# A fused attention and SwiGLU kernel: leftover tokens as half-size products, sums split between two engines, loads moved within a batch

## The chip, the cores and the metric

The kernel runs on one core of a Trainium2 chip. A core has a matrix engine (TensorE, PE in the profile, with PEld for its weight loads), a vector engine (VectorE, DVE), a scalar engine (ScalarE, ACT), a general engine (GpSimd, POOL) and a queue engine (SyncE, SP). Each runs its own instruction list in order and waits for others by semaphores. DMA transfers are issued from POOL, SP and ACT. The metric is the time of one execution in microseconds on the device: before the change a median of 237.15 us over three runs, 236.67 to 237.42.

## The reference

Eight batches, eight heads, 576 tokens, head size 64, 32 memories; then a SwiGLU block of width 512 with 1536 inner features over all 4608 tokens.

```python
def _attn_ref(q, k, v, phi):
    a = phi - np.max(phi, axis=2, keepdims=True)
    a = np.exp(a)
    a = a / (np.sum(a, axis=2, keepdims=True) + 1e-09)
    k_m = np.einsum('bhsm,bhsd->bhmd', a, k)
    v_m = np.einsum('bhsm,bhsd->bhmd', a, v)
    scores = (1.0 / np.sqrt(q.shape[-1])) * np.matmul(q, k_m.transpose(0, 1, 3, 2))
    attn = softmax(scores)
    return np.matmul(attn, v_m)

def _moe_ref(x, w_gate, w_val, w_out):
    g = x @ w_gate
    silu = g * (1.0 / (1.0 + np.exp(-g)))
    return silu * (x @ w_val) @ w_out
```

x is the attention's output with its heads side by side. Inputs and output are float32; the kernel computes in bfloat16 with float32 sums.

## The kernel before, in words

**A batch.** For batch b the kernel exponentiates phi (`phi_exp`), multiplies it with k and v (`kv_sum`, L235, into the tiles p_kv), divides by the column sums (`kv_denominators` L263, `kv_reciprocal`, `kv_norm` L271) and transposes the result into t_kT (`kv_T`). The values are folded into the gate and value weights (`u_round`, L471, evacuated to t_U by ScalarE L491 and VectorE L495). Scores come from q (transposed to t_qT by a DMA on SP) and t_kT (`scores`, L400); ScalarE takes their exponential (L411), VectorE sums and inverts it (`z_inv_v`: L434, L441, L443) and multiplies (`norm`, L451), once for each half g of the heads. This gives t_A, twice a batch.

**Slots.** The gate and value products of a batch run as 24 slots (12 blocks of 128 features, two halves of 288 tokens). `gv_gate` multiplies for the gate and ScalarE applies SiLU (t_sg, L531); one slot later the value product comes and VectorE multiplies both into t_h (L537). Three chunks c of four blocks make one tile t_h each. When a chunk is complete, `chunk_done` is called.

**Products.** The last multiplication, by w_out, uses a seven-product scheme for 2 x 2 blocks (four sums of activations, four of weights). It covers the first 512 of the 576 tokens of a batch: two halves of 256 tokens, with the features taken as even and odd blocks. `chunk_done` makes the activation sums t_S (L601 and, by `subtract`, L559: t[:, 0] = A21 + A22, t[:, 1] = t[:, 0] - A11, t[:, 2] = A11 - A21, t[:, 3] = A12 - t[:, 1]); for c = 0 and 1 GpSimd does this, for c = 2 VectorE. `products` lays out seven products of six units (a unit is two matmuls of 256 columns, L706): first (p1 and the one added to it), five, six, three, seven, four. They add up in the banks p_os, p_oa and p_oc, and `keep`, `c11`, `c22`, `c12`, `c21` copy and add them out and store them. A unit is not run at once: it goes into `backlog`, and `take(n)` runs the next n.

**Leftover tokens.** The last 64 tokens of each batch are copied by GpSimd (`ends`, L591) into xs of a pair of batches, t_x, 128 rows. `out_rest(pair, half)` multiplies them plainly by half of w_out: 12 matmuls of 256 columns in six units (L654), eight such passes in all.

**The order of the work** is written by hand. An iteration b of the last loop starts with 36 units of the former batch's products, with the scores, the softmax and `u_values` between them; then the 24 slots with what is spread between them: `kv_items(b + 1)` at slots 7 to 11 (with `u_item(b, 2)` behind it), `u_three(b + 1)` at 19 to 20, and the rest of the backlog from slot 4 on. GpSimd's list holds, in an iteration from 3 on: the loads of batch b + 2 (`loads`, L93, L98, L102, L115, four DMA issues), the last copy of leftover tokens, `phi_sum(b + 1)` (a sum over phi behind a mark that waits for t_A, L215 and L217, which makes the denominators two matmuls in place of nine), the sums and copy of c = 0, the sums and copy of c = 1. In iteration 2 the loads stand in the slots and there is no `phi_sum`. SP's list holds stores, the t_qT transposes and, from batch 4 on, the t_kT transposes. Eight banks of PSUM are handed out in order of release (`bank`, `done`).

Of the kernel before, what the change touches and what calls it, by code (L numbers as in the profile page):

```python
# [9 lines left out]
FP32 = mybir.dt.float32  # L10
# [4 lines left out]
def kernel(  # L15
# [193 lines left out]
    def phi_sum(b):  # L209

        e = ephis[b].rearrange("p j i m -> p j (i m)")
        mark = att.tile([1, 1], BF16, tag="mark", bufs=1, name="t_mark")
        nc.gpsimd.tensor_copy(out=mark, in_=atts[b - 1, 1][0:1, 0, 0:1])  # L215
        t = att.tile([128, 4, 128], FP32, tag="es", bufs=1, name="t_es")
        add = lambda o, x, y: nc.gpsimd.tensor_tensor(out=o, in0=x, in1=y, op=ALU.add)  # L217
        add(t, e[:, 0:4], e[:, 4:8])
        add(t[:, 0:2], t[:, 0:2], t[:, 2:4])
        add(t[:, 0], t[:, 0], t[:, 1])  # L220
        add(t[:, 0], t[:, 0], e[:, 8])
        hl = att.tile([128, 2, 128], BF16, tag="ehl", bufs=1, name="t_ehl")
        nc.gpsimd.tensor_copy(out=hl[:, 0], in_=t[:, 0])
        nc.gpsimd.tensor_tensor(out=hl[:, 1], in0=t[:, 0], in1=hl[:, 0], op=ALU.subtract)
        esums[b] = hl
# [71 lines left out]
    def kv_items(b, beside=None):  # L297


        def run_sums():  # L300
            o = 2 * D
            p = [bank([128, CH], FP32, f"p_kv{g}") for g in range(NG)]
            kv_denominators(b, p[0][:, o:o + NG])
            kv_sum(b, p, (0, 1))
            kv_reciprocal(b, p[0][:, o:o + NG])
            kv_norm(b, p)
            done(*p)
            if beside:
                beside()

        return [run_sums, lambda: kv_T(b)]
# [273 lines left out]
    def chunk_done(b, c):  # L585

        if b % 2 == 0 and c == 0:
            xs[b // 2] = hpool.tile([128, NJF, 2, 64], BF16, tag="xs", name="t_x")

        def ends():  # L590
            nc.gpsimd.tensor_copy(  # L591
                out=xs[b // 2][:, 4 * c:4 * c + 4, b % 2], in_=hts[b, c][:, :, S - 64:S]
            )

        t = upool.tile([128, 4, 2, 256], BF16, tag=f"U{c}" if b == 1 else f"S{c}", name="t_S")
        Ss[b, c] = t
        A11, A12, A21, A22 = blocks(b, c)

        def sums(eng, part=(0, 1, 2, 3)):
            if 0 in part:  # L600
                eng.tensor_tensor(out=t[:, 0], in0=A21, in1=A22, op=ALU.add)  # L601
            terms = ((t[:, 0], A11), (A11, A21), (A12, t[:, 1]))
            for n in part:
                if n:
                    subtract(eng, t[:, n], *terms[n - 1])

        end = c + 1 == NCH
        if (b, c) in ((0, 2), (1, 1), (1, 2)):
            late.append(lambda *part: sums(nc.gpsimd if b else nc.vector, *part))
        else:  # L610
            sums(nc.vector if end else nc.gpsimd)
        if end and b > 1:
            late.append(ends)
        else:
            ends()
        if (b, c) in beside_sums:
            beside_sums[b, c]()

# [4 lines left out]
    }  # L623

# [10 lines left out]
    def store(t_o, b, t0, count, row=0, cols=slice(0, 512), queues=None):  # L635

        if queues is None and box.get("end"):
            queues = nc.sync, nc.scalar
        for n, (r0, m, bb, jj, pp) in enumerate(token_segments(b, t0, count)):
            eng = queues[n % len(queues)] if queues else nc.sync  # L640
            eng.dma_start(out=out_r[bb, jj, pp:pp + m, cols], in_=t_o[row + r0:row + r0 + m])

    def out_rest(pair, half):

        h = DM // 2
        mine = {}
        cols = slice(h * half, h * half + h)

        def unit(n):
            def run():  # L650
                if n == 0:
                    mine["p"] = bank([128, h], FP32, "p_oo")
                for jf in (2 * n, 2 * n + 1):
                    nc.tensor.matmul(  # L654
                        mine["p"],
                        lhsT=xs[pair][:, jf].rearrange("p a t -> p (a t)"),
                        rhs=WO[jf][:, cols],
                        start=(jf == 0),
                        stop=(jf == NJF - 1),
                    )  # L660
                if n == NJF // 2 - 1:
                    t_o = work.tile([128, h], FP32, tag="to", name="t_o")
                    copy("v" if box.get("end") else "a", t_o, mine["p"])
                    done(mine["p"])
                    end = 2 * pair + 2 == B
                    for k in range(2):
                        store(
                            t_o, 2 * pair + k, S - 64, 64, 64 * k, cols,
                            ((nc.sync, nc.scalar)[k],) if end else None,
                        )  # L670

            return run

        return [unit(n) for n in range(NJF // 2)]

    def products(b, by_hand):
# [3 lines left out]
        lo, hi = slice(0, h), slice(h, DM)  # L680

        def A(e, n):
            return lambda c, m, u: hts[b, c][
# [3 lines left out]
        def Sx(n):  # L687
            return lambda c, m, u: Ss[b, c][:, n, m, 128 * u:128 * u + 128]
# [7 lines left out]
        def product(home, lhs, rhs, after):  # L696
            def unit(k):
                c, m = k // 2, k % 2

                def run():  # L700
                    fresh = k == 0 and home not in mine
                    if fresh:
                        mine[home] = bank([128, 2, h], FP32, f"p_o{home}")
                        mine[home, "new"] = True
                    for u in range(2):
# [21 lines left out]
        def keep(name, home):  # L727
            def run():
                nc.scalar.copy(out=tile_of(name, tag=name, bufs=1), in_=mine[home])
# [8 lines left out]
        def both(name, t0, cols):  # L738
            for u in range(2):
                store(mine[name][:, u, cols], b, t0 + 128 * u, 128, cols=cols)  # L740

        def c11():
            t = tile_of("o1", (128, 2, DM), tag="to")
            add(t[:, :, lo], "a", "p1", True)
            if box.get("end"):
                both("o1", 0, lo)

        def c22():
            t = tile_of("o2", (128, 2, DM), tag="to")
            add(t[:, :, hi], "s", "p5")  # L750
            if box.get("end"):
                both("o2", 256, hi)

        def c12():
            t = mine["o1"]
            add(t[:, :, hi], "c", "q6", True)
            both("o1", 0, hi if box.get("end") else slice(0, DM))

        def c21():
            t = mine["o2"]  # L760
            copy("v" if box.get("end") else "a", t[:, :, lo], mine["s"])
            done(mine["s"])
            both("o2", 256, lo if box.get("end") else slice(0, DM))
# [4 lines left out]
        )  # L768
        now = {n: f for n, f in ops.items() if n not in by_hand}
# [6 lines left out]
        if b + 1 == B:  # L776
# [177 lines left out]
    for b in range(2, B):  # L954
        last = b + 1 == B
        exp_tables()
        if b == 2:
# [15 lines left out]
            mark = att.tile([1, 1], BF16, tag="mark", bufs=1, name="t_mark")  # L973
            nc.gpsimd.tensor_copy(out=mark, in_=Ts[2][0:1, 3, 0, 0:1])
# [5 lines left out]
        else:  # L980
            backlog += out_rest(b // 2 - 1, b % 2)
            run(take(6))
        if b > 2:
            loads(b)
# [20 lines left out]
        if b == 2:  # L1005
            u_three(2)
            run(out_rest(0, 0))
            u_values(2)
            backlog = one[36:]
        g = gv_slots(b)  # L1010
        beside = 0 if last else min(7, len(backlog))
        outs = [lambda: run(take(1)) for _ in range(len(backlog) - beside)]
        streams = [(g, 0, 24), (outs, 4, 24)]
        if last:
            streams += [([u_item(b, 2)], 5, 6)]
        if not last:
            load_qT(b + 1)
            if b > 2:
                phi_sum(b + 1)
            else:  # L1020
                streams += [([lambda: loads(2)], 7, 8)]
            streams += [
                (kv_items(b + 1, lambda: (u_item(b, 2, "aava")(), run(take(2)))), KV, KV + 4),
                ([lambda: (run(take(2)), u_three(b + 1), run(take(3)))], 19, 20),
# [8 lines left out]
    run(out_rest(B // 2 - 1, 0))  # L1033
# [3 lines left out]
    run(backlog)  # L1037
    run(out_rest(B // 2 - 1, 1))
# [28 lines left out]
```

The softmax here doesn't subtract the row's maximum and nothing guards it: scores larger than these inputs give would overflow.

## Time and profile before

| what | us |
|---|---|
| median of three runs | 237.15 |
| the profiled execution | 236.3 |
| its span, first to last instruction | 234.5 |
| TensorE busy | 225.9 |
| VectorE busy | 187.4 |
| ScalarE busy | 172.5 |
| GpSimd busy | 135.2 |

The granted clock of TensorE was 1.000. Times below are microseconds from the span's start. A row of the timeline gives start, duration, engine, line, operation, what it writes and reads, and the number of instructions merged. A busy matrix engine in the rows is not one at its peak: its ends are modelled and neighbours overlap, so costs of matmuls are taken from the distance between starts. In the chain of waits twelve product matmuls of 256 columns stand at 1.31 and two slot matmuls of 288 columns at 0.24 or 0.25. The slots of batches 3 to 6 end (last value product) at 118.94, 144.17, 169.48 and 194.77, those of batch 7 at 218.37; the last matmul group, the second half of the last `out_rest`, starts at 228.85 and takes 1.32.

### The profile page before, as it was taken

The numbers are of one execution on the slowest core, as the hardware profiler recorded it, in microseconds if no ns is written. First come the engines' busy times: TensorE is split into PE (matmuls) and PEld (weight loads), VectorE is DVE, ScalarE is ACT, GpSimd is POOL, SyncE is SP. The second block draws the span as 40 slices with busy tenths as digits, with TensorE's granted clock in tenths as the row PEclk, the third lists the DMA queues.
The fourth block names the chain that finished last, engine by engine and source line by source line (L and its number), as shares of the span: only waits on it lengthen the run. The fifth ranks groups of instructions, "written<-read, shape, count | busy, mean of one in ns | idle before, by whom it ended". The sixth has DMA issues, their size and how long they took to land.

```text
span 234.5 us, 7300 instructions
## 1 busy us (share of the span) xinstructions
PE 225.9 (96%) x2847; PEld 171.3 (73%) x2847; DVE 187.4 (80%) x417; ACT 172.5 (74%) x368; POOL 135.2 (58%) x171
## 2 busy tenths in 40 slices
PE   7998899999999999999999999999999999999992
PEld 2555466778887777887778777877788777878881
DVE  4157699999979697998799878988799879987621
ACT  2758888988447888977898779968897789677310
POOL 8532426999099159654992399267916493029400
PEclk9999999999999999999999999999999999999999
DMA  6999999999974999899559964999313721122134
GB/s 211 205 205 207 198 208 206 228 238 248 207 169 97 252 216 158 166 247 232 137 80 252 214 110 106 225 226 142 110 25 81 132 89 27 31 62 89 33 92 126
DMA packets 42914, 36.84 MB, mean 157 GB/s; under 512 B 15488, under 2 KB 38528, under 8 KB 42880
## 3 DMA queue, kind: packets, MB, share of 16 engines
q0 software_dynamic: 21440, 22.42, 55.0%
q1 hardware_dynamic: 20176, 12.79, 25.8%
q10 hardware_dynamic: 1264, 1.18, 1.6%
q8 instruction: 22, 0.36, 0.6%
q14 instruction: 12, 0.10, 0.1%
HBM read 42.47 MB, written 9.44 MB: 221 GB/s over the span
## 4 chain that ended last, share of the span: by engine, by line
PE 82%; DMA 8%; POOL 4%; DVE 3%; issue 1%; ACT 0%; DVEq 0%; POOLq 0%
PE p_g L514 20%; PE p_v L514 19%; PE p_os L706 16%; PE p_oc L706 8%; DMA t_kv<-in_v_dram 8%; PE p_u L471 5%; PE p_oo L654 5%; PE p_oa L706 4%; PE p_kv L235 2%; POOL t_es L217 1%; POOL t_q L108 1%; PE p_g L400 1%; POOL t_kv L98 1%; DVE t_lz L443 1%; DVE t_z L434 1%
## 5 line engine op out<-in xcount | busy, mean ns | idle before, releaser
L537 DVE TENSOR_TENSOR t_h<-t_sg,p_v 128x288 bf16<-128x288 bf16 x192 | 83.1, 452 | 15.6 <-PE p_v L514 7.6
L514 PEld LDWEIGHTS <-t_U 128*128 128x128 bf16 x768 | 73.7, 98 | 21.7 <-issue 2.9
L531 ACT ACTIVATE t_sg<-p_g 128x288 bf16<-128x288 f32 x192 | 74.5, 423 | 15.9 <-PE p_g L514 9.1
L514 PE MATMUL p_g<-t_A,t_U 128*128 128x288 bf16 x384 | 77.2, 286 | 0.0
L514 PE MATMUL p_v<-t_A,t_U 128*128 128x288 bf16 x384 | 77.0, 286 | 0.0
L706 PEld LDWEIGHTS <-t_S 128*128 128x128 bf16 x384 | 37.4, 98 | 4.5 <-issue 0.2
L601 POOL TENSOR_TENSOR t_S<-t_h 128x512 bf16<-128x512 bf16 x17 | 19.7, 1156 | 35.2 <-DVE t_h L537 35.2
L491 ACT CAST t_U<-p_u 128x512 bf16<-128x512 f32 x53 | 28.0, 608 | 8.9 <-PE p_u L471 8.9
L706 PEld LDWEIGHTS <-t_h 128*128 128x128 bf16 x288 | 27.3, 98 | 7.8 <-issue 4.0
L706 PE MATMUL p_os<-t_T,t_S 128*128 128x256 bf16 x192 | 23.7, 273 | 0.0
L559 POOL TENSOR_TENSOR t_S<-t_S,t_h 128x512 bf16<-128x512 bf16 x17 | 19.6, 1155 | 1.3
L559 POOL TENSOR_TENSOR t_S<-t_h,t_S 128x512 bf16<-128x512 bf16 x17 | 20.1, 1186 | 0.0
L559 POOL TENSOR_TENSOR t_S<-t_h 128x512 bf16<-128x512 bf16 x17 | 19.6, 1155 | 0.0
L471 PE MATMUL p_u<-W,t_kT 64*32 64x512 bf16 (+1 forms) x416 | 15.9, 363 | 0.1
L706 PE MATMUL p_os<-t_T,t_h 128*128 128x256 bf16 x96 | 15.6, 273 | 0.0
L827 PE MATMUL p_warm<-bones 128*128 128x512 bf16 (+2 forms) x43 | 12.9, 427 | 1.7 <-DVE bones L850 1.7
L451 DVE TENSOR_TENSOR t_A<-t_E,t_lz 128x576 bf16<-128x576 bf16 x16 | 13.4, 840 | 0.9 <-ACT t_lz L427 0.3
L654 PE MATMUL p_oo<-WO,t_x 128*128 128x256 bf16 x96 | 14.0, 273 | 0.0
L495 DVE CAST t_U<-p_u 128x512 bf16<-128x512 f32 x19 | 12.4, 683 | 1.6 <-PE p_u L471 1.6
L215 POOL COPY t_mark<-t_A 1x1 bf16<-1x1 bf16 x4 | 0.7, 182 | 20.3 <-DVE t_A L451 20.3
L706 PE MATMUL p_oc<-t_T,t_S 128*128 128x256 bf16 x96 | 12.0, 273 | 0.0
L706 PE MATMUL p_oa<-WO,t_h 128*128 128x256 bf16 x96 | 11.8, 273 | 0.0
(93 smaller groups left out, 309.9 us busy)
## 6 DMA issues: line engine op xcount, KB each, us to landing
t_kv<-in_k_dram POOLq DMA_DIRECT2D x8, 576.0 KB, 10.1
t_kv<-in_v_dram POOLq DMA_DIRECT2D x8, 576.0 KB, 14.4
out_dram<-t_o SPq DMA_DIRECT2D x21, 192.0 KB, 2.6
t_phi<-in_phi_dram POOLq DMA_DIRECT2D x6, 576.0 KB, 7.9
t_q<-in_q_dram POOLq DMA_DIRECT2D x5, 576.0 KB, 7.4
out_dram<-t_o SPq DMA_DIRECT2D x37, 64.0 KB, 2.0
out_dram<-t_o SPq DMA_DIRECT2D x14, 128.0 KB, 5.8
t_q<-in_q_dram POOLq DMA_DIRECT2D x6, 288.0 KB, 11.3
```

The source lines that it names most:

```text
L451: nc.vector.tensor_tensor(out=a, in0=es.pop((b, g)), in1=lzs.pop((b, g)), op=ALU.mult)
L471: nc.tensor.matmul(p[g][32 * i:32 * i + 32, o:o + n], lhsT=kTs[b][64 * g:64 * g + 64, 2, 32 * i:32 * i + 32], rhs=w_part(w, c, i, g, halve ...
L491: nc.scalar.copy(out=t, in_=p)
L495: nc.vector.tensor_copy(out=t, in_=p)
L514: nc.tensor.matmul(p[:, 0:HALF], lhsT=Us[b, c, g][:, o // 2, which, 128 * (o % 2):128 * (o % 2 + 1)], rhs=atts[b, g][:, r], start=(g == 0) ...
L531: nc.scalar.activation(out=sg, in_=gate[:, 0:HALF], func=AF.Silu)
L537: nc.vector.tensor_tensor(out=dst, in0=sg, in1=val[:, 0:HALF], op=ALU.mult)
L559: eng.tensor_tensor(out=out, in0=x, in1=y, op=ALU.subtract)
L601: eng.tensor_tensor(out=t[:, 0], in0=A21, in1=A22, op=ALU.add)
L654: nc.tensor.matmul(mine["p"], lhsT=xs[pair][:, jf].rearrange("p a t -> p (a t)"), rhs=WO[jf][:, cols], start=(jf == 0), stop=(jf == NJF - 1),)
L706: nc.tensor.matmul(mine[home][:, u], lhsT=lhs(c, m, u), rhs=rhs(c, m), start=fresh and u == 0, stop=(k == 5), skip_group_check=u == 1 or n ...
L827: nc.tensor.matmul(p[:, 0:128 * a], lhsT=bones, rhs=x.to_broadcast([128, a, 128]) if a > 1 else bones, start=True, stop=True,)
```

## The change

- `out_rest` is gone. The leftover tokens of four batches (two pairs, 256 rows) form a "quad" and go through the seven-product scheme too: `products(b, by_hand, quad)` with one matmul a unit, 42 a quad. `quad_sums` makes their activation sums on GpSimd: four per chunk, of 256 elements each, one of them in place in t_x; the tiles are t_Q. Quad 0 (batches 0 to 3) has its sums in batch 3 and its products in batch 4: twelve units ahead of the slots, thirty spread over slots 0 to 6. Quad 1 has its sums in batch 7; twelve of its units lie in batch 7's slots, twelve behind `three` of the last products and eighteen at the very end.
- From batch 2 on GpSimd makes t[:, 0] and t[:, 1] of c = 1 when the chunk is done (in batches 3 and 7 also of c = 0 no more than these); a mark (`wait_for`) then holds it until VectorE's sums of c = 2 are through, and the other two follow. Their order is t[:, 3] first, in batch 7 t[:, 2] first.
- `loads(b)` moves from the start of iteration b (in iteration 2, from slots 7 to 8) to the end of chunk 0 of batch b, behind a mark on t_h and ahead of that chunk's sums.
- `kv_items`: the denominators from `phi_sum` come after `kv_sum`, `u_item` and two units; the reciprocal and the normalisation come after them in every case. Batch 5 has no `phi_sum`.
- In iteration 2 the last six units of batch 1's products stand between `u_three` and `u_values`, where `out_rest(0, 0)` was; no units are left for its slots. At most four units in place of seven are kept for `kv_items` and `u_three`, and `u_three` is followed by two units in place of having two before and three behind it.
- The stores at the end alternate between SP and ACT by a running count (`turn`).

```diff
         end = c + 1 == NCH
+        fourth = b in (3, 7)
         if (b, c) in ((0, 2), (1, 1), (1, 2)):
             late.append(lambda *part: sums(nc.gpsimd if b else nc.vector, *part))
+        elif b < 2:
+            sums(nc.gpsimd)
+        elif end:
+            sums(nc.vector)
+            wait_for(t[0:1, 3, 0, 0:1])
+            for part in ((2,), (3,)) if b + 1 == B else ((3,), (2,)):
+                for f in second:
+                    f(nc.gpsimd, part)
+            second.clear()
         else:
-            sums(nc.vector if end else nc.gpsimd)
-        if end and b > 1:
+            if c == 0:
+                wait_for(hts[b, 0][0:1, 3, 0:1])
+                loads(b)
+            if c or fourth:
+                sums(nc.gpsimd, (0, 1))
+                second.append(sums)
+            else:
+                sums(nc.gpsimd)
+        if end and b > 1 and not fourth:
             late.append(ends)
         else:
             ends()
+        if fourth and c != 1:
+            quad_sums(b // 4, (0,) if c == 0 else (1, 2))
...
+    def wait_for(x):
+        t = att.tile([1, 1], BF16, tag="mark", bufs=1, name="t_mark")
+        nc.gpsimd.tensor_copy(out=t, in_=x)
+
+    def quad_sums(qd, chunks):
+        x, y = xs[2 * qd], xs[2 * qd + 1]
...
+        for n in range(4):
+            for c in chunks:
+                t = Qs[qd, c]
+                A11, A12, A21, A22 = quarters(c)
+                if n == 0:
+                    nc.gpsimd.tensor_tensor(out=t[:, 0], in0=A21, in1=A22, op=ALU.add)
+                elif n == 1:
+                    subtract(nc.gpsimd, t[:, 1], t[:, 0], A11)
+                elif n == 2:
+                    subtract(nc.gpsimd, A21, A11, A21)
+                else:
+                    subtract(nc.gpsimd, t[:, 2], A12, t[:, 1])
...
         def run_sums():
             o = 2 * D
             p = [bank([128, CH], FP32, f"p_kv{g}") for g in range(NG)]
-            kv_denominators(b, p[0][:, o:o + NG])
+            if b not in esums:
+                kv_denominators(b, p[0][:, o:o + NG])
             kv_sum(b, p, (0, 1))
+            if beside:
+                beside()
+            if b in esums:
+                kv_denominators(b, p[0][:, o:o + NG])
             kv_reciprocal(b, p[0][:, o:o + NG])
             kv_norm(b, p)
             done(*p)
-            if beside:
-                beside()
...
         else:
-            backlog += out_rest(b // 2 - 1, b % 2)
             run(take(6))
-        if b > 2:
-            loads(b)
...
         if b == 2:
             u_three(2)
-            run(out_rest(0, 0))
+            run(one[36:])
             u_values(2)
-            backlog = one[36:]
         g = gv_slots(b)
-        beside = 0 if last else min(7, len(backlog))
+        quad = []
+        if b == 4:
+            quad = products(b, (), 0)[0]
+            run(quad[:12])
+        if last:
+            rest, rest_ops = products(b, (), 1)
+            backlog += rest[:12]
+        beside = 0 if last else min(4, len(backlog))
         outs = [lambda: run(take(1)) for _ in range(len(backlog) - beside)]
-        streams = [(g, 0, 24), (outs, 4, 24)]
+        streams = [(g, 0, 24), (quad[12:], 0, 6), (outs, 6 if quad else 4, 24)]
...
             load_qT(b + 1)
-            if b > 2:
+            if b > 2 and b != 4:
                 phi_sum(b + 1)
-            else:
-                streams += [([lambda: loads(2)], 7, 8)]
             streams += [
                 (kv_items(b + 1, lambda: (u_item(b, 2, "aava")(), run(take(2)))), KV, KV + 4),
-                ([lambda: (run(take(2)), u_three(b + 1), run(take(3)))], 19, 20),
+                ([lambda: (u_three(b + 1), run(take(2)))], 19, 20),
             ]
...
     run(take(6))
     ops["p1"]()
-    run(out_rest(B // 2 - 1, 0))
     box["end"] = True
     run(take(6))
     ops["c11"]()
-    run(backlog)
-    run(out_rest(B // 2 - 1, 1))
+    run(backlog[:24] + rest[12:24] + backlog[24:] + rest[24:])
```

## The prediction

> **What bounds the kernel now.** I read the page's first and fourth parts, then busy time by stage, then the timeline round the ends of two batches. Names: c0, c1, c2 are a batch's three chunks; A0 and A1 are VectorE's two normalisations (L451); U is the moment when the matmuls of `u_three` (L471 x24, near a batch's end) are through.
>
> ```profile
> PE 225.9 (96%) x2847; PEld 171.3 (73%) x2847; DVE 187.4 (80%) x417; ACT 172.5 (74%) x368; POOL 135.2 (58%) x171
> ...
> PE 82%; DMA 8%; POOL 4%; DVE 3%; issue 1%; ACT 0%; DVEq 0%; POOLq 0%
> ```
> TensorE is the limit: 82% of the chain of waits is its own.
>
> ```profile
> core 0: us, PE busy (x) PEld busy (x) DVE busy (x) ACT busy (x) POOL busy (x), PEclk, DMA share, GB/s
> ...
> 127.49:144.17 16.68, 16.68 (x236) 12.72 (x235) 13.96 (x33) 13.40 (x33) 12.89 (x16) 1.00 0.83 160
> 144.17:152.72 8.55, 8.55 (x99) 7.19 (x97) 8.19 (x16) 7.47 (x13) 3.80 (x8) 1.00 0.95 180
> ```
> The first row is one batch's gate/value slots, the second the stretch of products before the next batch's first gate. In the second TensorE is full, but VectorE is busy 8.19 of 8.55: it runs the sums of c2, the softmax sums, A0 and A1, and the first gate reads A0 and A1. So there are two nearly equal chains, TensorE's and VectorE's. The next view shows them change places, at the end of batch 2:
>
> ```profile
> 91.91 0.63 ACT L331 COPY t_o<-p_os 128x512 f32<-128x512 f32 x1
> 92.39 1.38 ACT L531 ACTIVATE t_sg<-p_g 128x288 bf16<-128x288 f32 x4
> ...
> 94.47 0.42 DVE L601 TENSOR_TENSOR t_S<-t_h 128x512 bf16<-128x512 bf16 x1
> ...
> 97.85 0.90 DVE L451 TENSOR_TENSOR t_A<-t_E,t_lz 128x576 bf16<-128x576 bf16 x1
> ...
> 101.19 0.76 DVE L451 TENSOR_TENSOR t_A<-t_E,t_lz 128x576 bf16<-128x576 bf16 x1
> 101.69 0.83 PE L514 MATMUL p_g<-t_A,t_U 128*128 128x288 bf16 x4
> ```
> U is 90.36 here (the chain of waits shows the last L471 at 89.59 for 0.77). ScalarE's copy of the last product falls behind the four casts of `u_three` and pushes the last four activations to 92.39. VectorE's sums start at U+4.11, A1 ends at 101.95, U+11.59, and the four gate matmuls take 0.83 instead of 0.65 (the same four at 127.32): TensorE waited 0.18. Later batches do that copy before `u_three` and do not wait. So VectorE has no slack left in this pattern.
>
> The third thing to see is what GpSimd does to VectorE (the timeline):
>
> ```profile
> 69.04 2.78 POOL L559 TENSOR_TENSOR t_S<-t_h,t_S 128x512 bf16<-128x512 bf16 x2
> 69.52 1.29 DVE L451 TENSOR_TENSOR t_A<-t_E,t_lz 128x576 bf16<-128x576 bf16 x1
> ...
> 71.78 2.26 POOL L559 TENSOR_TENSOR t_S<-t_h 128x512 bf16<-128x512 bf16 x2
> ...
> 73.24 1.42 DVE L451 TENSOR_TENSOR t_A<-t_E,t_lz 128x576 bf16<-128x576 bf16 x1
> ```
> A0 takes 0.76 in a quiet place (123.23) and 1.29 and 1.42 here. The times fit one instruction waiting for the other: GpSimd's first subtraction ends at 69.04 + 1.11 = 70.15, A0 ends 0.66 later at 70.81, and the GpSimd pair takes 2.78 where the undisturbed pair takes 2.26, since its second waited for A0. In the next two rows GpSimd ends at 74.04 and A1 0.62 later.
>
> **The change, part by part.** All against the profiled execution: 236.3 us, span 234.5. The median is 237.15, 0.85 above; I add the sum to the median.
>
> *Matmuls.* Eight passes of 12 (96) become two times seven products of 6 (84). Twelve matmuls of 256 columns take 1.31 in the chain, 0.109 each: **-1.31**. By place: -18 before the tail, +6 in it. I name no cover, since TensorE is full from 54 us on.
>
> *Denominators.* Batch 5 loses its GpSimd pre-sum and has nine matmuls for two; nine took 81.33 - 81.00 = 0.33, so 7 x 0.037 = **+0.26**. Elsewhere they move behind the key/value sums, `u_item` and two units, some 1.8 us later, and the wait for t_ehl, 0.6 in three batches in the list of waits, is gone: **-0.6** (0 if GpSimd is late too).
>
> *Ends of batches 3 to 6.* With `out_rest` gone only six units are left for the slots: two beside the key/value sums, two loose, two after `u_three`. So the copy of the last product comes behind the casts, the order of batch 2 above. That costs that batch's wait at the last value matmuls (92.59 in place of 92.21 + 0.25, taken as 0.15), the sums at U+4.11, and a first gate without slack: it wants A1 at U+11.45, which is when an A1 with nothing in its way ends (11.59 less the 0.14 by which A0 at 97.85 was slowed).
>
> *GpSimd after VectorE's sums.* Now `wait_for` holds two of c1's subtractions until c2's sums end; 0.2 for the mark, 1.11 and 1.11 follow. A0 starts 1.91 after the softmax reduction (97.85 - 95.94), so the second subtraction, which ends 2.4 after the sums, stands in its way: A0 waits 0.6, and so does the gate. Bounds: 0 (sums early, activations late) to 0.66 (the slower row above). I take 0.6. Behind that mark queue c1's S3 and S2, the t_x copy and the next pre-sum; the products want S3 and S2 at U+9.15 and U+10.46 and get them by 9.3 at the latest for S2, and the pre-sum waits for A1 anyway. Batch 6 to 7 has only this: 0.6 + 0.15 = **+0.75**.
>
> *Loads past c0's sums.* Four DMA issues take 3.08 of GpSimd (119.05 to 122.13). In batches 2 to 5 they now stand, behind a mark, between c0's last multiplication and c0's sums, and every sum, t_x copy and (batch 3) quad sum queues behind them. Batch 4: c0 to VectorE's sums is 134.49 to U = 140.99, 6.50, less 0.56 of work gone from the stretch, plus 4.11: 10.05; the reciprocal now follows the later denominators, so c0 may be 0.5 later: 9.55. GpSimd needs 0.14 + 3.08 + 4.55 (four sums) + 0.36 + 2.35 (c1's first two) = 10.5. [...] With A0's 0.6: 1.33 to 1.83, I take 1.6, + 0.15, for 4 to 5 and for 5 to 6: **+3.5**. Bounds: 0 (GpSimd clear and nothing late) and 2.0. If the loads stood where they do now there would be 3 us of slack.
>
> [...]
>
> *Batch 2 to 3.* No product matmuls are left in these slots, and no copy behind the casts: U comes 0.88 sooner (two groups of 0.44), VectorE's sums could start at U+3.63 (4.11 less 0.48 of copy), and the gate wants A1 at U+11.02 (0.44 fewer matmuls after U). From c0 to those sums there are 90.36 - 84.36 - 0.88 + 3.63 = 8.75, or 8.25 with c0 late, against the same 10.5: two sums and the copy are interleaved with VectorE's four. Ended at 7.0 to 7.5 after U in place of 5.1; A1 5.87 after that and 0.6: 13.5 to 14.0, so 2.45 to 2.95 late, I take 2.65 less the 0.2 that was there: **+2.45** (0 to 2.95).
>
> *Batch 3 to 4.* Here both chunks keep two subtractions and eight quad sums follow. A quad sum has 256 elements; rows: a 256 copy 0.40, a 256 f32 sum 0.73, a 512 sum 1.15. A fixed 0.15 (from 0.44 and 0.73 for 128 and 256) and the rest by size gives 0.65, spaced 0.61. The twelve quad matmuls ahead of the slots give 1.31 of cover for A1. But S3 and S2 of c1 come at U+9.7 and U+12.5, wanted at 9.15 and 10.46; the products wait 2.1 (1.6 with c0 early), and the six quad units reach their third sum 0.5 too soon. **+2.4** (0 to 3.0).
>
> *Tail.* From the last value matmul (218.37): VectorE's sums end at +2.2, mark +0.2, four sums 4.46, copy 0.36: quad sums start at +7.2. `six` needs the fourth of them, +9.65; TensorE, with 76 matmuls ahead, is there at 8.3 and has only `five`, `four` and the rest after it. Wait with the hand-over: **+1.4**; 0.6 (0.40 each) to 1.9 (0.73 each).
>
> *Without cost.* The stores' `turn` and the quads' eight stores: SP's queue has gaps, and what follows them, the transpose t_kT, lands in 3.6 to 4.6 (3.9 median); it is issued some 1.9 after the sums' round and wanted 6.9 after it. The loads' own data land in 7.9 to 14.4, wanted 12 us or more after issue. If that cover goes, `u_three` waits, up to 1 us a batch.
>
> *Sum:* -1.31 + 0.26 - 0.6 + 0.75 + 3.5 + 2.45 + 2.4 + 1.4 = **+8.85**: span 243.35, time 246.0.
>
> **The rivals.**
> *GpSimd is clear of VectorE's sums* (its issues overlap more than I read, or c0 comes earlier). Then the four collisions go and A0's wait stays: 0.75 three times, 1.0 for 3 to 4, 0.4 for 2 to 3, tail 1.4, less 1.65: +3.4, 240.5. For it: GpSimd misses by 1 us in 10. Against: every one of those durations repeats within 0.05 in the trace.
> *Faster:* the second halves fit between VectorE's sums and A0 and no gate waits; then only -1.65 and the tail's shortest wait 0.6: -1.05, 236.1. It decides at U+4.1: c1's first half must be through by then, and the sums must end 0.6 before the softmax reduction can start, as they would if ScalarE were not late. Against it: the order on ScalarE.
> *No change:* the waits at the ends come to about 1.65 and nothing more, 237.2.
> *Loads meet the transposes:* t_qT took 9.27 with loads in flight (79.03) and 3.05 without (180.91); if t_kT grew so, `u_three` waits 1 us in three batches on top of the forecast: 249.
> That the change does not do what it says is excluded for the matmuls: they are counted.
>
> **How the numbers follow.** Forecast 0.55, clear port 0.20, transposes 0.05: slower 0.80. No change 0.07. Faster 0.13. A difference of 0.3% (0.7 us) is about what a measurement of this kernel can tell. The forecast's own range, by its bounds, is 242 to 248.7; to leave out no more than 0.2 the range reaches down through the clear port, 239, and up to 249.
>
> **What would show it.** Right: VectorE's first sum of c2 (L603) over 0.8 long in batches 2 to 5; A0 over 1.2; the first four gate matmuls spread by over 1 us; TensorE idle ahead of p_os from t_Q in the tail by about 1.4. Wrong: GpSimd idle before its mark for t_S in batches 4 and 5, or the copy of t_o ahead of the casts. The prediction falls if A1 still ends before TensorE wants it.

## The result, and the profile after

The changed kernel takes 263.0 us (median of four runs, 261.8 to 264.67) against 236.91 (four runs of the kernel before beside it): a ratio of 1.1104, interval 1.1036 to 1.1173. It is slower by 26.1 us, where 246.0 and at most 249 had been predicted. The profiled execution took 261.8, its span is 260.0.

The page's first and fourth parts, kernel after:

```profile
PE 231.3 (89%) x2842; PEld 171.8 (66%) x2842; DVE 191.0 (73%) x423; ACT 174.1 (67%) x368; POOL 149.0 (57%) x200
...
PE 52%; DMA 19%; DVE 15%; POOL 5%; issue 4%; ACT 2%; ACTq 1%; DVEq 0%; SPq 0%; POOLq 0%
```

TensorE's share of the chain fell from 82% to 52%, and DMA's rose from 8% to 19%: a transfer is now waited for in mid-kernel. The list of waits (engine, line, what it waits for: us in total, times, longest) says which:

```profile
POOL t_mark L645 <- DVE t_S L561: 36.0, 6, 10.3
...
PE p_u L473 <- DMA t_kT<-t_bkv: 15.4, 3, 6.0
```

`u_three` (L473) waits 15.4 us for the DMA transposes t_kT in batches 3, 4 and 5, the batches in which loads are issued. (Batches are counted by the iteration here and in the experiments: iteration 3 makes t_kT for batch 4, and so on.) The first line belongs to a step of the prediction: GpSimd sits idle at the mark ahead of the second halves, so it is not late. That is the sign of being wrong that the prediction named. The timeline of the first stall:

```profile
107.47 0.81 POOL L115 DMA_DIRECT2D t_q<-in_q_dram  x1 [0.36 <-issue]
...
109.36 2.04 SPq L288 DMA_TRANSPOSE t_kT<-t_bkv  x1
...
109.80 0.75 POOL L102 DMA_DIRECT2D t_kv<-in_v_dram  x1
...
118.81 1.48 PE L473 MATMUL p_u<-W,t_kT 64*32 64x512 bf16 x24 [4.43 <-DMA t_kT<-t_bkv]
```

The same stretch in the kernel before, where the loads go out 13 us sooner and v, the last of them, lands at 110.7:

```profile
94.64 0.81 POOL L115 DMA_DIRECT2D t_q<-in_q_dram  x1 [0.43 <-issue]
...
104.65 6.00 SPq L121 DMA_TRANSPOSE t_qT<-t_q  x1
110.76 1.65 SPq L289 DMA_TRANSPOSE t_kT<-t_bkv  x1
...
114.91 0.84 PE L471 MATMUL p_u<-W,t_kT 64*32 64x512 bf16 x24
```

In the kernel after, t_kT is issued among the four loads and lands 9.4 us later; it took 3.6 to 4.6 before. Without loads (batch 6) it takes 3.1 here. In batch 4, which has the longest of the waits, the quads' stores add to it:

```profile
141.54 1.20 SPq L699 DMA_DIRECT2D out_dram<-t_p  x2
142.83 3.67 SPq L699 DMA_DIRECT2D out_dram<-t_q  x4
146.61 1.28 SPq L288 DMA_TRANSPOSE t_kT<-t_bkv  x1
```

VectorE has t_bkv, which t_kT reads, ready at 144.58, but six stores stand ahead on SP's queue and t_kT goes out 2.0 later.

And the 24 matmuls behind the wait take 1.48, where they took 0.84 in the same view before. Busy time by stage (columns as in the prediction) shows why:

```profile
118.81:122.00 3.19, 3.19 (x32) 1.52 (x33) 1.38 (x2) 2.50 (x6) 0.00 (x0) 0.50 1.19 203
122.00:126.00 4.00, 4.00 (x53) 2.94 (x52) 3.39 (x9) 3.29 (x8) 0.00 (x0) 0.98 0.51 140
```

The third number from the right, 0.50, is the granted clock: half speed for the 3.2 us after the stall, 0.98 after that. After the stalls that end at 155.68 and 186.95 it is 0.50 to about 159.5 and 190.4. Some 10.5 us at half speed lose up to 5 more (an estimate, half of the three stretches together).

The end of batch 5, which answers to the end of batch 2 shown before:

```profile
192.95 0.42 DVE L603 TENSOR_TENSOR t_S<-t_h 128x512 bf16<-128x512 bf16 x1
...
194.57 0.18 POOL L645 COPY t_mark<-t_S 1x1 bf16<-1x1 bf16 x1 [8.80 <-DVE t_S L561]
...
195.82 1.14 POOL L561 TENSOR_TENSOR t_S<-t_h 128x512 bf16<-128x512 bf16 x1
196.46 1.46 DVE L453 TENSOR_TENSOR t_A<-t_E,t_lz 128x576 bf16<-128x576 bf16 x1
```

VectorE's sums run undisturbed (0.42), but A0 takes 1.46 in place of 0.76: GpSimd's second late subtraction stands in its way, as predicted.

Some kernels below have executions 3 to 8 us longer than their others, at a lower mean clock; their times are given, and the ratios leave them out.

### The profile page after: what moved, and what is told of

Read it like the earlier page. It is cut to its first block, busy times and chain, and to the rows that moved or that the text cites. A ratio compares the mean times of both kernels' runs of the same rounds, so it can differ in the third digit from the quotient of the medians.

```text
span 260.0 us, 7337 instructions
## 1 busy us (share of the span) xinstructions
PE 231.3 (89%) x2842; PEld 171.8 (66%) x2842; DVE 191.0 (73%) x423; ACT 174.1 (67%) x368; POOL 149.0 (57%) x200
## 4 chain that ended last, share of the span: by engine, by line
PE 52%; DMA 19%; DVE 15%; POOL 5%; issue 4%; ACT 2%; ACTq 1%; DVEq 0%; SPq 0%; POOLq 0%
PE p_g L516 16%; PE p_v L516 15%; DMA t_kT<-t_bkv 11%; PE p_os L739 10%; DMA t_kv<-in_v_dram 7%; PE p_u L473 5%; DVE t_lz L445 3%; DVE t_z L436 3%; PE p_oc L739 3%; DVE t_o L769 2%; POOL t_S L561 2%; DVE t_A L453 2%; DVE t_h L539 2%; PE p_kv L234 2%; DVE t_S L561 1%
## 5 line engine op out<-in xcount | busy, mean ns | idle before, releaser
L539 DVE TENSOR_TENSOR t_h<-t_sg,p_v 128x288 bf16<-128x288 bf16 x192 | 81.6, 450 | 18.5 <-PE p_v L516 8.8
L516 PEld LDWEIGHTS <-t_U 128*128 128x128 bf16 x768 | 75.0, 99 | 25.9 <-issue 6.2
L533 ACT ACTIVATE t_sg<-p_g 128x288 bf16<-128x288 f32 x192 | 75.3, 419 | 21.5 <-PE p_g L516 13.8
L516 PE MATMUL p_g<-t_A,t_U 128*128 128x288 bf16 x384 | 79.2, 290 | 2.1 <-DVE t_A L453 2.1
L516 PE MATMUL p_v<-t_A,t_U 128*128 128x288 bf16 x384 | 78.0, 289 | 0.1
L473 PE MATMUL p_u<-W,t_kT 64*32 64x512 bf16 (+1 forms) x416 | 17.8, 405 | 15.4 <-DMA t_kT<-t_bkv 15.4
L645 POOL COPY t_mark<-t_S 1x1 bf16<-1x1 bf16 x6 | 1.1, 179 | 36.0 <-DVE t_S L561 36.0
L473 PEld LDWEIGHTS <-t_kT 64*32 64x32 bf16 x416 | 5.3, 94 | 20.6 <-DMA t_kT<-t_bkv 16.3
L453 DVE TENSOR_TENSOR t_A<-t_E,t_lz 128x576 bf16<-128x576 bf16 x16 | 17.2, 1078 | 0.7 <-ACT t_lz L429 0.3
L645 POOL COPY t_mark<-t_h 1x1 bf16<-1x1 bf16 x6 | 1.1, 179 | 23.1 <-DVE t_h L539 23.1
```

The lines of the kernel that those rows point to most:

```text
L453: nc.vector.tensor_tensor(out=a, in0=es.pop((b, g)), in1=lzs.pop((b, g)), op=ALU.mult)
L473: nc.tensor.matmul(p[g][32 * i:32 * i + 32, o:o + n], lhsT=kTs[b][64 * g:64 * g + 64, 2, 32 * i:32 * i + 32], rhs=w_part(w, c, i, g, halve ...
L516: nc.tensor.matmul(p[:, 0:HALF], lhsT=Us[b, c, g][:, o // 2, which, 128 * (o % 2):128 * (o % 2 + 1)], rhs=atts[b, g][:, r], start=(g == 0) ...
L533: nc.scalar.activation(out=sg, in_=gate[:, 0:HALF], func=AF.Silu)
L539: nc.vector.tensor_tensor(out=dst, in0=sg, in1=val[:, 0:HALF], op=ALU.mult)
```

## The experiments

The first theory was that the loads delay t_kT. Three kernels tried it and its rivals; a fourth tried a repair in the tail.

**Loads back.** Edit to the kernel after:

```diff
-            if c == 0:
-                wait_for(hts[b, 0][0:1, 3, 0:1])
-                loads(b)
...
+        if b > 2:
+            loads(b)
         for g in range(NG):
             scores(b, g)
...
+            if b == 2:
+                streams += [([lambda: loads(2)], 7, 8)]
```

> The kernel after with one part undone: the loads of batch b+2 go back to the places they had before (start of the iteration for batches 3 to 5, eighth slot for batch 2), with no mark ahead of them. Theory A (the loss is the DMA transposes t_kT caught behind the loads, and the slow clock after each stall): t_kT lands in 3.6 to 4.6 us again, the 15.4 us wait of TensorE for it is gone, u_three's 24 matmuls take about 0.77 instead of 1.48, and 263.0 - 15.4 - some 6 for the clock = 241.6; range 239 to 243. Rival B (GpSimd's order and the quad sums cost it, the loads little): above 250. Rival C (my terms of the prediction less the loads: -1.65 + 0.75 x 3 + 0.4 + 1.0 + 1.4 = +3.4): 240.3, inside A's range.

Measured 262.61 (260.5 to 263.47), ratio 1.1076 (1.1035 to 1.1118): nothing gained, and theory A as stated falls. The timeline says why:

```profile
98.36 0.81 POOL L115 DMA_DIRECT2D t_q<-in_q_dram  x1
...
105.19 9.06 SPq L121 DMA_TRANSPOSE t_qT<-t_q  x1
114.36 1.46 SPq L288 DMA_TRANSPOSE t_kT<-t_bkv  x1
...
118.76 1.02 PE L473 MATMUL p_u<-W,t_kT 64*32 64x512 bf16 x24 [4.44 <-DMA t_kT<-t_bkv]
```

"Back" in the program is not back in time. In GpSimd's list the loads now follow the wait for VectorE's sums, so they go out at 98.36 instead of 94.64. They meet t_qT, which holds SP's queue for 9.06 (6.00 before), and t_kT, behind it in that queue, is issued at 114.36 instead of 110.76. In batch 4 the six stores of the quad's results come on top: they wait behind t_qT and hold the queue from 146.65 to 150.87, t_kT goes out at 150.98, and TensorE waits 7.13, the longest of the three waits (4.44, 7.13, 4.28).

**Only the loads moved**, in the kernel before:

```diff
+            if b > 1 and c == 0:
+                mark = att.tile([1, 1], BF16, tag="mark", bufs=1, name="t_mark")
+                nc.gpsimd.tensor_copy(out=mark, in_=hts[b, 0][0:1, 3, 0:1])
+                loads(b)
...
-        if b > 2:
-            loads(b)
...
-            else:
-                streams += [([lambda: loads(2)], 7, 8)]
```

> The kernel before with one part alone: the loads of batch b+2 stand behind a mark ahead of c0's sums, as in the kernel after; out_rest, whole c1 sums and everything else stay. Theory A: t_kT lands in 9 to 10 us in the batches with loads, TensorE waits 12 to 18 us for it and runs slow after each stall: 236.9 + 18 to 22 = 255 to 259. Rival B (the loads do harm only together with the halved sums and the quads): 236 to 240.

253.21 (250.39 to 254.53), ratio 1.071 (1.0665 to 1.0755), somewhat below theory A's range: by the medians the loads alone cost 16.3. The profiled execution, at 250.39 the shortest of the four, has 9.5 us of wait for t_kT, which lands in 10.4, 9.0 and 10.0.

**t_kT on TensorE**: in `kv_T`, `if b > B:` in place of `if b > 3:`.

> The kernel after with the loads where the change put them, but the three t_kT transposes of every batch on TensorE (as batches 2 and 3 do) instead of by DMA. Theory A: no DMA is waited for, three TensorE transposes and a VectorE copy in four batches add under 1 us each; 263.0 - 21.4 + 1 to 3 = 242 to 245. Rival B (what costs is GpSimd's 3 us of load issues and the sums behind them): still above 250. If the loads ahead of c0's sums also cost by VectorE's collisions, as I predicted (some 6 us over three ends), this run stays that much above the one with the loads put back.

244.47 (244.11 to 244.96), ratio 1.0324 (1.0289 to 1.0359). With the loads where the change put them and no DMA to wait for, 18.5 of the 26.1 us are gone.

**A buffer for c11.** In the tail of the kernel after, ScalarE's copy to t_p waits 2.79 for a store of the quad's result, which lies in the same single buffer, and TensorE waits 0.77 and 0.73 behind it. Edit, on the kernel with the loads back: `t = work.tile([128, h], FP32, tag="to", name="t_o")` for c11 in `leftover`.

> The kernel after with the loads put back, and the quads' c11 result in a buffer of its own (tag to) instead of the second half of p1's only buffer. Theory (the copy of the main p1 in the tail waits 2.79 us for that result's store, and TensorE 0.77 and 0.73 behind it): 0.8 to 1.5 us below the run with only the loads back. Rival (TensorE has other products to do in that time, or the quad sums come just as late): within 0.3 of it.

263.27 (262.05 to 264.08), ratio 1.1116 (1.108 to 1.1152): nothing gained, which is nearer the rival. From the last `u_three` to the end it takes 46.8 where "loads back" takes 47.1. The list on TensorE in the tail:

```profile
248.36 1.47 PE L736 MATMUL p_os<-t_T,t_S 128*128 128x256 bf16 x12 [0.81 <-POOL t_S L561]
...
251.70 0.39 PE L736 MATMUL p_os<-t_T,t_Q 128*128 128x256 bf16 x2 [0.35 <-POOL t_Q L561]
252.33 0.39 PE L736 MATMUL p_os<-t_T,t_Q 128*128 128x256 bf16 x2 [0.23 <-POOL t_Q L561]
```

The wait for the store had hidden the wait for GpSimd; taking it away shows 0.81 + 0.35 + 0.23 = 1.39 behind it.

So theory A': what counts is when loads are issued against t_qT and t_kT. Four kernels varied that.

**Loads ahead of the wait.** With the loads back, `loads(b + 1)` at the end of iteration b, before `wait_for`:

```diff
             sums(nc.vector)
+            if b >= 2:
+                loads(b + 1)
             wait_for(t[0:1, 3, 0, 0:1])
```

> The kernel after, with the loads of batch b+2 issued at the end of the iteration before, ahead of the wait for VectorE's sums and of the second halves (some 92 to 95 us for the first of them, where the kernel with the loads put back behind that wait issued them at 98.4 and the kernel before at 94.6). Theory A' (a DMA transpose that has to share with loads in flight is slow; what counts is when the loads are issued against t_qT and t_kT): t_qT lands in 9 or less, t_kT in 3.6 to 4.6, TensorE's wait for it is gone: 262.6 - 15.8 - some 6 for the clock = 239.5 to 242. Rival D (the quads' stores ahead of t_qT on SP's queue, or the halved sums, delay the transposes, not the loads): t_kT still waited for by over 10 us in all, above 250.

244.19 (five runs 243.86 to 244.77, one 252.24), ratio 1.0315 (1.0282 to 1.0348). 18.4 us come back with halved sums, quads and stores as they are, so rival D falls as the main cause; 2.2 above the range that was written down. t_kT lands in 3.4, 2.4 and 3.7; only batch 3 waits, 1.68.

**Sums whole**: the same with `sums(nc.gpsimd)` for c = 0 and 1, no wait.

> The same without the halving: GpSimd does all four sums of c1 (and of c0 in batches 3 and 7) at once, no wait for VectorE's sums, loads at the end of the iteration before; the quads and the moved denominators stay. Theory: A0 no longer waits for GpSimd's late subtractions (0.6 by my prediction at four ends), the gates start up to 0.6 sooner there, products never wait for c1's S2 and S3: 1.5 to 3.5 below the run with the loads ahead and the sums halved, 237 to 239. [...]

244.83 (five runs 243.87 to 245.87, one 248.66), ratio 1.0324 (1.0286 to 1.0362): no gain in all, but by intervals (table below) batches 4 and 5 gain 0.47 and 0.60 and batch 3 loses 2.87, where quad sums now queue behind all of c0's and c1's (A1 takes 3.46 there, 1.28 with the sums halved). So the halving costs time in batches 4 and 5, as the theory has it, and saves time in batch 3.

**Half the loads moved**: q and phi ahead of the wait, k and v where the change put them.

> The kernel after, with q's and phi's loads (1152 of 2304 KB) issued at the end of the iteration before, and only k's and v's where the change put them. Theory A' with the bytes in flight as the dose: t_kT lands in 5 to 7.5 instead of 9 to 10, TensorE waits 3 to 9 us in all instead of 15.4, 245 to 253. Rival (any load in flight costs the same, as with a queue that is switched): t_kT 9 to 10 and the time still above 258. Rival (the order on GpSimd matters, not the loads): above 258 too, with t_kT late by its issue.

263.51, 265.41, 268.43 and 270.23; ratio 1.1172 (1.1107 to 1.1236): a miss, no better than the kernel after. The profile is of the longest of these. t_kT lands in 8.0, 8.5 and, by the end of TensorE's wait, 10.0, so half the bytes save 0 to 1.4 us a batch, not 2 to 5; TensorE's waits for it are 11.5 instead of 15.4. But q's new load now waits 6.8 for t_qT to have read the buffer it overwrites, with everything behind it on GpSimd, and TensorE waits 4.5 for t_qT.

**One mark**, in the kernel before:

```diff
         if b > 2:
+            mark = att.tile([1, 1], BF16, tag="mark", bufs=1, name="t_mark")
+            nc.gpsimd.tensor_copy(out=mark, in_=Ss[b - 1, 2][0:1, 3, 0, 0:1])
             loads(b)
```

> The kernel before with one instruction more: a mark on GpSimd ahead of the loads of batches 3 to 5, which waits for VectorE's sums of c2, so that these loads are issued some 3 to 4 us later and nothing else changes. Theory A': they meet t_qT and t_kT, t_qT lands in 12 to 13 instead of 9.3, t_kT is issued late or lands late, TensorE waits for it in two or three batches and runs slow after it: 245 to 258. Rival (3 us of delay are absorbed, the halved sums or the quads are needed for the loss): 236 to 239.

240.05 (239.55 to 240.24), ratio 1.0137 (1.0101 to 1.0173), 5 below theory A's lower end. Timeline:

```profile
99.21 0.75 POOL L102 DMA_DIRECT2D t_kv<-in_v_dram  x1
...
104.77 8.40 SPq L121 DMA_TRANSPOSE t_qT<-t_q  x1
...
113.27 1.19 SPq L289 DMA_TRANSPOSE t_kT<-t_bkv  x1
...
116.69 0.84 PE L471 MATMUL p_u<-W,t_kT 64*32 64x512 bf16 x24 [1.52 <-DMA t_kT<-t_bkv]
```

The loads go out 2.2 us later than before (99.21 against 96.97), not 3 to 4. t_qT leaves SP's queue 2.5 later, t_kT is issued 2.5 later, and TensorE waits 1.52, after which the 24 matmuls still take 0.84. The kernel before had 1 us of slack here. The next two batches wait 1.80 and 0.50, together 3.8; the kernel is 3.6 slower than before.

Two kernels went the other way: loads later still, and a plain copy.

**Loads behind c0's sums**: in the kernel after, `loads(b)` below the sums, no mark.

> The kernel after, with the loads behind c0's sums instead of ahead of them: some 4.6 us later still (112 instead of 107.5). Theory A' (a transpose lands with the loads that were issued before it, and is fast when it is issued first): t_kT is issued about 109.4, before them, lands in 3 to 5, TensorE does not wait for it: 243 to 247, though the loads are later than in the kernel after. Rival E (any overlap of the two, or the loads' lateness itself, costs): 255 or more. Rival F (what counts is GpSimd's c0 sums coming 3 us late): same as the runs without transposes, 244.

246.47 (246.33 to 246.86), ratio 1.0404 (1.037 to 1.0438). Timeline:

```profile
167.27 1.18 SPq L288 DMA_TRANSPOSE t_kT<-t_bkv  x1
...
172.20 0.81 POOL L115 DMA_DIRECT2D t_q<-in_q_dram  x1
...
176.87 1.16 POOL L561 TENSOR_TENSOR t_S<-t_S,t_h 128x512 bf16<-128x512 bf16 x1
177.24 1.07 DVE L603 TENSOR_TENSOR t_S<-t_h 128x512 bf16<-128x512 bf16 x1
...
181.35 1.58 DVE L453 TENSOR_TENSOR t_A<-t_E,t_lz 128x576 bf16<-128x576 bf16 x1
```

In batch 3 the loads go out 5.8 us later than in the kernel after, and in all 16.5 us are gained: t_kT is issued first and lands in 2.4 to 3.0. Rival E falls. In this kernel the collision that I had predicted for the change does happen: c1's sums, behind 3.1 us of issues, reach into VectorE's, the first of which takes 1.07; gates wait up to 1.8.

**A plain copy**: `nc.sync.dma_start(out=kTs[b], in_=t)` in place of the transposing DMA.

> The kernel after with t_kT moved by a plain DMA of the same 96 KB on the same queue instead of a transposing one (so kT is not transposed in batches 4 to 7, which the computation leaves out). [...] Rival G (SP's transfers as a whole wait until the loads are through): 8 to 10 us and about 260.

256.11 in one run. The copy lands in 8.1, 7.7 and 7.2 behind loads and in 3.0 without; the transpose took 9.4, 9.0 and 10.0, and 3.1 without. So it is not mainly the transposition that is slow: rival G's 8 to 10 us and 260 are near. That SP's transfers as a whole wait until the loads are through is not shown: the first copy is done at 117.3, v, issued at 109.63, lands 13.6 later.

The first DMA t_kT by kernel (batch 3; loads: first issue, and v's issue plus its landing time):

| kernel | loads | t_qT in SP's queue | t_kT issued, lands in | TensorE waits |
|---|---|---|---|---|
| before | 94.64 to 110.7 | 104.65 to 110.65 | 110.76, 3.6 | 0 |
| one mark | 96.89 to 113.2 | 104.77 to 113.17 | 113.27, 3.4 | 1.52 |
| loads back | 98.36 to 115.7 | 105.19 to 114.25 | 114.36, 4.4 | 4.44 |
| after | 107.47 to 122.9 | 105.23 to 108.18 | 109.36, 9.4 | 4.43 |
| behind c0's sums | 113.28 to 129.5 | 106.45 to 109.47 | 110.58, 3.0 | 0 |

t_qT, where loads are in flight, leaves the queue about when the last of them has landed. t_kT of the kernel after, issued among them, is done at 118.8, 4 us ahead of the last; a t_kT issued ahead of them (3.0), or when they have landed (3.4 and 3.6, and 4.4 in "loads back"), is quick.

Four kernels looked at the 7 us that stay.

**The repairs together**: loads ahead, sums whole but in batch 3, batch 4's t_kT on TensorE, the buffer for c11.

> Four repairs at once: loads at the end of the iteration before, GpSimd's sums whole everywhere but in batch 3 (halved there, as the halved order was 2.9 us quicker over that batch's end), batch 4's t_kT on TensorE, and the quads' c11 result in a buffer of its own. From the run with whole sums (244.8): -2.9 for batch 3, -1.8 for the wait for t_kT less 0.5 for TensorE's transposes, -1.5 for the waits on t_p and t_q in the tail: 239.1; range 237.5 to 241. If the parts add up as I read them it is still not below 236.5, since twelve fewer matmuls are worth 1.3 and batch 3's end and the tail keep 1 to 2 us each. Rival (the tail is bound by GpSimd's sums, so that the own buffer gives nothing, as before): 240 to 242.

Three runs of 241.82 to 241.93 and three of 248.7 to 249.38; ratio 1.0208 (1.017 to 1.0247). The first three are 0.8 to 0.9 above the range written down, where the rival put them: TensorE still waits 1.8 in the tail for ScalarE's t_q. Nothing here beats the kernel before.

**No quads**: the kernel before with halved sums, later denominators and loads ahead.

> The kernel before with the halved sums of c1, the later denominators and the loads ahead of the halved part, but without quads: out_rest as before. Theory: what the quads cost is what is between this and the run with all of them and the loads ahead (244.2): batch 3's end 1.2 to 1.5, the tail 1.9 to 2.6, and the copy behind the casts in batches 3 to 6, less 1.3 for matmuls. The halving alone costs 0.55 at up to four ends, but here ScalarE is not late, so less: 236.5 to 239.5. Rival (the halving and the moved denominators are what costs, the quads nothing): 242 to 245.

243.41 (241.67 to 245.13), ratio 1.0276 (1.0231 to 1.0322): the rival's number by another road. With `out_rest` kept, batch 7's copy of leftover tokens queues behind the halved sums, a wait that neither kernel has:

```profile
PE p_oo L673 <- POOL t_x L594: 3.0, 1, 3.0
```

Without that wait it would be at some 240.4 (an estimate, 243.41 less 3.0), about 3.8 below the run with the quads and the loads ahead.

**Late denominators alone**, in the kernel before (the change's edit of `run_sums`, nothing else):

> The kernel before with one part alone: the denominators, reciprocal and normalisation behind the key/value sums, u_item and two units. My prediction: the 0.6 us of waits for t_ehl go, 236.3. Rival (the normalisation, and with it t_kT or TensorE's transposes of it, come later than they are wanted; in the kernel after TensorE waits 0.56 for t_bkv in batch 2): 237 to 239.

236.85 (235.86 to 239.19), ratio 1.0013 (0.9986 to 1.0039): no difference. By intervals, read as in the table below, the profiled run gains 0.1 to 0.15 in each of three batches; in batch 3 it waits 1.56 for t_kT. There the loads, issued at 94.52 (94.64 in the kernel before), land 2.8 later (113.4), and t_kT goes out 2.5 later (113.22).

**Halved sums alone**: as "no quads", with the denominators as before and batch 7's copy ahead of the wait.

> The kernel before with GpSimd's sums of c1 halved round VectorE's, the loads ahead of the wait for these, and batch 7's copy of leftover tokens ahead of it too (in the run without quads it stood behind, and TensorE waited 3.0 us for t_x at the end); no quads, denominators as before. My prediction for the halving: 0.6 at each of four ends by the wait of A0, without the 0.15: 239.3; range 238 to 240. Rival (nothing of it reaches TensorE, since here the copy of the last product is ahead of the casts and A1 has slack): 236.5 to 237.5. Rival (the loads' place costs as well, by t_qT and t_kT): 241 or more.

239.89 (239.57 to 240.01), ratio 1.0137 (1.0116 to 1.0159), in the range written down. The end of batch 4:

```profile
174.34 0.18 POOL L618 COPY t_mark<-t_S 1x1 bf16<-1x1 bf16 x1 [4.45 <-DVE t_S L559]
...
175.60 1.14 POOL L559 TENSOR_TENSOR t_S<-t_h 128x512 bf16<-128x512 bf16 x1
176.23 1.47 DVE L451 TENSOR_TENSOR t_A<-t_E,t_lz 128x576 bf16<-128x576 bf16 x1
```

A0 takes 1.47, 0.71 more, and each of the four ends is 0.7 to 0.9 longer, although the copy of the last product is ahead of the casts here.

From `u_three` to `u_three`, and from the last to the span's end, read off the timelines. The columns count `u_three` by the batch that it is made for, so "3 to 4" holds the end of batch 2, and so on to "6 to 7" with the end of batch 5; "to the end" holds those of batches 6 and 7:

| kernel | 3 to 4 | 4 to 5 | 5 to 6 | 6 to 7 | to the end |
|---|---|---|---|---|---|
| before | 25.39 | 25.24 | 25.30 | 25.30 | 43.75 |
| after | 28.90 | 36.87 | 31.27 | 25.95 | 47.10 |
| t_kT on TensorE | 24.83 | 30.51 | 25.04 | 25.05 | 46.96 |
| loads ahead | 25.61 | 29.91 | 24.98 | 24.95 | 47.12 |
| sums whole | 25.98 | 32.78 | 24.51 | 24.35 | 46.69 |
| halved sums alone | 26.28 | 26.01 | 26.02 | 25.98 | 43.90 |

## Why the prediction was wrong, step by step

**Where the 26.1 us are.** 18.5 are the loads upon t_kT, undone in two ways (244.47 and 244.19); 3.1 the halved sums alone; 0 the denominators alone. The 4.3 to 4.6 that are left fall, by subtraction and shown by no run of its own, to the quads and the order of units round them, after the 1.3 that twelve fewer matmuls save. "No quads", less its wait for t_x, gives 3.8 for the same by another subtraction.

**"Without cost", the step that failed.** I wrote that t_kT lands in 3.6 to 4.6, and that `u_three` waits up to 1 us a batch if that cover goes. The waits were 4.43, 5.98 and 4.98, 15.4 in all, and the clock fell to 0.50 after each. In the profiled executions the span falls by 17.6 with t_kT on TensorE and by 17.5 with the loads ahead, for 15.4 and 13.7 of these waits: the slow clock's part is about 2 to 4. The rival "Loads meet the transposes" named the place and had the row (t_qT 9.27 with loads in flight, 3.05 without), and I gave it 1 us and a chance of 0.05. What I did not do is lay the loads' landing times over t_kT's issue: before, v landed at 110.7 and t_kT went out at 110.76; the change puts t_kT 1.9 us behind the first of four loads that take 15 us to land. From t_qT's 6 us of excess and some 3 us of slack (6.9 wanted, 3.9 taken) 3 us a batch could have been worked out. Measured slack was smaller: t_kT was wanted 5.0, 3.1 and 5.0 after issue, not 6.9. Two other parts of the change had taken it, which I had put at nothing for t_kT: with the denominators moved, t_bkv is ready 3.1 after the key/value sums start (106.23 to 109.30), where it was 2.0 before (131.41 to 133.45); and in batch 4 the quads' stores hold SP's queue 2.0 longer. The clock was not in the sum at all.

**GpSimd into VectorE's sums (4 to 5, 5 to 6, part of 2 to 3).** Wrong place. The mark on t_h reads a token of the chunk's last block but of its first half, so it opens one slot sooner than I took it to, and c1's first two sums end ahead of VectorE's. The kernel after has room there by its stalls alone; "t_kT on TensorE" has no such stalls and shows the same: at the end of batch 5 the mark opens at 162.57, ahead of the chunk's last multiplication (164.86), GpSimd's sums end at 173.51, VectorE's first starts at 175.40 and takes 0.43, and GpSimd then sits idle at its mark for 3.17. "T_kT on TensorE" and "loads ahead" agree within 0.1 at these two ends (columns 5 to 6 and 6 to 7), so the loads' place costs nothing through GpSimd there. The 1.0 an end that the +3.5 has beyond A0's 0.6 and the 0.15 no run of the change shows: VectorE's first sum takes 0.42 in all of batches 2 to 5. Nor does a run show the port that the chances speak of; what is shown, with the loads behind c0's sums, is a sum of VectorE's drawn out to 1.07 beside a GpSimd sum of 1.16.

**A0's wait, 0.6.** Right: 0.70 in the rows above, 0.48 three times and 0.82 twice in "t_kT on TensorE", 0.47 and 0.60 by "sums whole" against "loads ahead". Where it is alone an end costs 0.7 to 0.9, about 0.6 + 0.15, though the copy order that the 0.15 stood for is not in that run.

**Batch 2 to 3, +2.45.** Too much: 24.83 against 25.39 (column 3 to 4), about 0.75 of waits with 1.3 of matmuls gone. A term I had none for stands one stage sooner: U comes 0.4 to 0.5 later, not 0.88 sooner, and TensorE waits 0.56 there for t_bkv, with no units left to fill slots.

**Batch 3 to 4, +2.4.** Column 4 to 5, 30.51 less 25.24, less 30 matmuls (3.27) and 0.26: 1.7, within the bounds.

**Tail, +1.4, with 6 to 7, +0.75.** "To the end" grew by 3.35; less 0.65 of matmuls 2.7, against 2.15. I missed the store that ScalarE's t_p waits for; the wait for GpSimd that I had priced at 1.4 lies behind it and came out at 1.39 once it was free. That the two numbers agree is partly luck: 0.58 of it is for t_Q, as I had said, and 0.81 for t_S, which I had not.

**Matmuls and denominators.** The matmuls are as said, within what the intervals can show. Of the 0.6 for the denominators the run with them alone shows 0.1 to 0.15 in three batches and nothing in its time. All terms but the failed one make +8.85; without that one's cause the runs show +7.5 to +7.7. The sum was nearly right by luck, with errors of both signs: too much at the ends of batches 2 to 5, too little in the tail, for U and for the denominators. The range was missed by one step.

## What to carry to other kernels

When a bulk load is moved, list every small transfer that something waits for and ask which of them it will now be in flight with: a transfer issued just behind the loads can wait for most of their flight (9.4 us here for one that takes 3.1 alone), so either it goes out ahead or the loads land before it (2.4 to 4.6 here, both ways). Putting a line back does not put it back in time if a wait has been added ahead of it on that queue. A wait that is taken away often uncovers the one behind it.

## What the runs showed of the hardware

- SP's t_qT instruction, issued while loads are in flight, stayed in its queue about as long as they were: 3.0 us without them, 6.0, 8.4 and 9.06 with (before, "one mark", "loads back"), ending within 1.5 us of the last landing. What was behind it in the queue was issued only then (t_kT 0.1 us later in all three).
- A plain copy of 96 KB suffers nearly as much as a transpose (7.2 to 8.1 against 9.0 to 10.0, alone 3.0 and 3.1), and half the bytes in flight help little (8.0, 8.5, 10.0). The copy needs fewer packets (q1 moves 3120 between 100 and 130 us, and 3392 in the kernel after for the same list of transfers) and gains only 1.3 to 2.8 us. How the transfers in flight are served is not shown.
- After each of the three waits for t_kT in the kernel after (4.43, 5.98 and 4.98) the clock was 0.50, for 3.2 to 3.9 us. Over the runs, read off the 24 matmuls of `u_three`, how surely they came slow went with the length of that wait: those of 0.50 to 1.80, 2.42 and 3.01 us left them at 0.84, one of 2.24 made it 1.30; from 3.12 to 4.44 the result was 0.84, 0.86, 0.99, 1.02 or (six times) 1.48 or 1.47, from 4.98 on always 1.47 or 1.48. What decides between them, when a wait of 2.24 ("a plain copy") is followed by slow matmuls and one of 3.30 ("only the loads moved") by none, is not shown.
